# A recurrence and a gated MLP on one core: x through DRAM, state copies on ScalarE, u on four tiles, paired lane groups, and an order that counts queue time

## The chip, the cores and the metric

The kernel runs on one core of a Trainium2 chip. The core has five engines with a queue of instructions each: TensorE (PE; its weight loads are shown as PEld), VectorE (DVE), ScalarE (ACT), GpSimd (POOL) and SyncE (SP). Here SP issues every DMA. The metric is the device time of one execution in microseconds; the time before is the median of three runs.

## What is computed

Two parts in a row. First a recurrence over 768 tokens, for 4 batches and 8 heads of dimension 40:

```python
for t in range(S):
    y[:, :, t] = np.einsum('bhd,bhde->bhe', rt, state)
    Sa = np.einsum('bhde,bhe->bhd', state, at)
    state_decay = state * wt[:, :, None, :] - np.einsum('bhd,bhe->bhde', Sa, bt)
    state = state_decay + np.einsum('bhd,bhe->bhde', vt, kt)
```

Then y, reshaped to x of 3072 tokens by 320, goes through a gated product: `a = x @ w_a; b = x @ w_b; out = (a * b) @ w_out`, with d_ff = 1536. All in float32; the weights come in a wide form that is decoded on the chip.

## The kernel before

**Chunks.** The 768 tokens are cut into 12 chunks of 64 (`C`). A chunk is worked on in two pairs c = 0, 1 (two batches each, `NP`), so there are 24 steps. In a chunk the recurrence is solved with matrices, in these stages:

- `prep(n, c)` (line 506) loads w, b/k and a (tiles W, BK, A), scales them by running products on DVE (Q, pe), makes the `scores` on PE, copies them to AB and TK, and transposes BK (`nat`, tile bkn). A, pe, TK and bkn are written to a DRAM tensor `un_d[q]`.
- `lanes(g)` (line 600) inverts the triangular 32 x 32 blocks of a group of chunks: one transposition of AB, 31 steps of two DVE operations on tiles Y, Yt and N, two transpositions back. `GROUPS` (line 40) says which chunks share one such inverse; a group costs the same whether it holds one chunk or two. `merge` (line 632) completes the inverse of a chunk, tile T; four DMAs copy its diagonal blocks (`T<-TC`).
- `main(n, c)` (line 687) is the step itself. It loads UN (all of `un_d[q]` in one transfer), v into half of SV, and r and v (RV). On PE: `r_`, `u_` (line 716; u in two layouts), `s_`, `g_`, `y_`, and a transposition of the state. On ACT and DVE the results go to RH, SV, uT, tmp, ST, G, SD. `s0` (line 752) copies the state ST to SV for the next chunk by four DMAs of 40 partitions. Last, DVE makes X (one buffer), ACT rounds it to XH, POOL forms the rest X - XH in X.
- `packh` and `packl` (lines 797, 804) move XH and X into the K-tiles `xk` of the second part, 120 partitions with three heads each, by six DMAs each from SBUF to SBUF.

**The second part.** One `unit` (line 410) is one chunk with one of the 12 weight tiles of 128 columns of d_ff: 16 matmuls into ab, a product on DVE, a split on ACT and POOL (gh, gl), 6 matmuls into po. The first four weight tiles (`F1`) are used chunk by chunk beside the recurrence. Each xk is also written to `xk_d[n]`; when the recurrence's buffers are free, all xk and the partial sums (`po_d`) are loaded again and the other eight tiles run over all chunks.

**What sets the order.** The code does not run its steps as written. `Plan.op` (line 84) notes each with its engine, an assumed length, its tiles and a rank v; `Plan.run` (line 116) places them: again and again, of the operations that could start earliest, the one of lowest rank is emitted. Each engine then runs what it was given, in that order. Every DMA is planned on SP with a length of 0.06 (0.12 to 0.36 for several) and a fixed time to landing of 2.5 to 5, whatever else is under way:

```python
pl.op("SP", 0.06, lambda: nc.sync.dma_start(out=UN, in_=un_d[q]), [("un", q, i) for i in range(5)], [kU], lat=4.0, v=v - 0.3)
pl.op("SP", 0.24, s0, [kST], [kS], lat=2.6)
pl.op("SP", 0.36, packh, [kXH], [("xkh", n % 2, c)], lat=2.6, v=v + 0.15)
```

All engine calls pass through one helper, so in the profile nearly every instruction carries line 58; the tiles' names tell them apart.

Of the kernel before, what the change touches and what calls it, by code (L numbers as in the profile page):

```python
# [18 lines left out]
B = 4  # L19
H = 8  # L20
D = 40
# [3 lines left out]
M = 8  # L25
# [14 lines left out]
GROUPS = ((0,), (1, 2), (3, 4), (5, 6), (7, 8), (9, 10), (11,))  # L40
# [4 lines left out]
KHEADS = ((0, 1, 6), (2, 3, 7), (4, 5))  # L45
# [18 lines left out]
class Op:  # L64
    __slots__ = ("eng", "dur", "fn", "deps", "users", "v", "lat", "need", "free", "mode", "end", "left", "ready", "seq")
# [9 lines left out]
class Plan:  # L75
# [40 lines left out]
    def run(self, slack=0.05, switch=0.13):  # L116
        engines = {e: 0.0 for e in ("PE", "DVE", "ACT", "POOL", "SP", "-")}
        busy = dict.fromkeys(engines, 0.0)
# [10 lines left out]
        while todo:  # L129
# [126 lines left out]
def wkv_moe(ctx, tc, wd, ai, bk, rvf, vn, pin, rv, wa, wb, wo, out):  # L256
# [48 lines left out]
    xk_d = [dram.tile([PK, 6, B * C], F32, name=f"xk_d{n}") for n in range(NS)]  # L305
    po_d = [dram.tile([2, P, DM], F32, name=f"po_d{n}") for n in range(NS)]
# [19 lines left out]
    def decode(i, src, rows, ncol, dst_hi, dst_lo, split):  # L326
# [10 lines left out]
        if not WIDE:  # L337
            yield "SP", 0.06, lambda: nc.sync.dma_start(out=raw, in_=src), (), (kr,), 3.0
# [7 lines left out]
        yield "SP", 0.06, lambda: nc.sync.dma_start(  # L346
            out=raw.rearrange("p c x -> p (c x)"), in_=src.bitcast(I32)), (), (kr,), 3.5
# [44 lines left out]
    def plan_tile(f, w, slot, v):  # L392
        for i, j, (eng, dur, fn, r, wr, lat) in tile_steps(f, w):
            kw = {"lat": lat} if lat else {}
# [5 lines left out]
        pl.op("SP", 0.12, lambda: fill_rows(w[0]), [("wt", slot, j) for j in range(2)],  # L400
              [("wf", slot)], v=v, lat=2.5)
# [79 lines left out]
    RH_ = ring(a1, 2, [P, M, D], "RH")  # L481
# [5 lines left out]
    XH_ = ring(a1, 1, [P, 4, 2 * C], "XH", F32R)  # L487
# [3 lines left out]
    for t in (AB, *T_, *ST_, *SV_, D1):  # L491
# [14 lines left out]
    def prep(n, c, v):  # L506
# [4 lines left out]
        un = un_d[q]  # L511
# [3 lines left out]
        pl.op("SP", 0.06, lambda: nc.sync.dma_start(out=W, in_=wd[n, c]), w=[kW], lat=2.6)  # L515
        pl.op("SP", 0.06, lambda: nc.sync.dma_start(out=BK.rearrange("p m x t -> p (m x t)"), in_=bk[n, c]), w=[kBK], lat=3.5)
        pl.op("SP", 0.06, lambda: nc.sync.dma_start(out=A.rearrange("p m t -> p (m t)"), in_=ai[n, c]), w=[kA], lat=2.6)
# [28 lines left out]
        def ak(gq):  # L546
            for j in range(2):
                nc.sync.dma_start(out=AKd[half(gq), gq, j],
                                  in_=A[half(j), gq * 4:gq * 4 + 4].rearrange("p i t -> p (i t)"))
        for gq in range(2):  # L550
            pl.op("SP", 0.12, lambda gq=gq: ak(gq), [kA], [("un", q, gq)], lat=2.6, v=v + 0.3)
        pl.op("SP", 0.06, lambda: nc.sync.dma_start(
            out=un[:, 16 * C:16 * C + CW], in_=PEt.rearrange("p m t -> p (m t)")), [kPE], [("un", q, 2)], lat=2.6, v=v + 0.3)
# [3 lines left out]
        def scores(ps=ps):  # L557
            for i in range(4):
                for kind in range(2):
                    for gq in range(2):  # L560
                        for j in range(2):
                            m, r = mi(gq, i), hd(j)
                            c0 = (kind * 4 + i) * C
                            mul(AT[half(gq ^ kind), ps.first + j, c0:c0 + C], BK[r, m, gq ^ kind], A[r, m])
        pl.op("PE", 1.86, scores, [kBK, kA], need=ps, mode="q", lat=0.1, w=[("sc", q), kAB, kTK])
# [17 lines left out]
        pl.op("SP", 0.12, tk, [kTK], [("un", q, 3)], lat=2.6, v=v + 0.3)  # L583
# [7 lines left out]
        pl.op("PE", 0.86, nat, [kBK], need=ps, mode="t", lat=0.1, w=[("nt", q), kBN])  # L591
# [4 lines left out]
        pl.op("SP", 0.06, lambda: nc.sync.dma_start(  # L596
            out=un[:, 16 * C + CW:], in_=BN.rearrange("p m j d -> p (m j d)")), [kBN], [("un", q, 4)], lat=2.6, v=v + 0.3)
# [34 lines left out]
    def merge(n, x, v):  # L632
# [16 lines left out]
        else:  # L649
            pl.op("SP", 0.24, diag, [("TC", x)], kT[0:2], lat=5.0)  # L650
# [7 lines left out]
        pl.op("PE", 1.05, l2a, kab + [("T3", x)], [("l3", n), "W4"], need=ps, mode="h", lat=0.1)  # L658
# [13 lines left out]
        pl.op("PE", 1.05, l2b, ["W4", ("TC", x)], [("l4", n), kT[2]], need=ps, mode="h", lat=0.1)  # L672
# [7 lines left out]
    def load_v(n, c, v):  # L680

        def go():
            for h in range(2):
                nc.sync.dma_start(out=SV_[c][half(h), 1 - h].rearrange("p j i d -> p (j i d)"), in_=vn[n, c, half(h)])
        pl.op("SP", 0.12, go, w=[("svv", c)], lat=2.6, v=v)

    def main(n, c, v):
# [7 lines left out]
        pl.op("SP", 0.06, lambda: nc.sync.dma_start(out=UN, in_=un_d[q]), [("un", q, i) for i in range(5)], [kU], lat=4.0, v=v - 0.3)  # L695
# [4 lines left out]
        pl.op("SP", 0.06, lambda: nc.sync.dma_start(  # L700
            out=RV.rearrange("p x m t -> p (x m t)"), in_=rvf[n, c]), w=[kRV], lat=3.0, v=v - 0.2)
# [3 lines left out]
        def r_(ps=ps):  # L705
            for j in range(2):
                for i in range(4):
                    for gq in range(2):
                        k = (j * 4 + i) * D
                        mul(AT[half(gq), ps.first, k:k + D], AK[:, gq, j, i], SV[:, gq, j, i])  # L710
        pl.op("PE", 0.95, r_, [kS, kV, kU], [("r", q), kRH], need=ps, mode="c", lat=0.1)
        pl.op("ACT", act(320), lambda ps=ps: nc.scalar.mul(
            out=RH.rearrange("p m d -> p (m d)"), in_=bank(ps, 0, slice(0, 8 * D)), mul=-1.0), [("r", q)], [kRH], free=[ps])
        ps = Banks(2)

        def u_(ps=ps):
            for m in range(M):
                for h in range(2):
                    mul(AT[half(h), ps.first, m * D:(m + 1) * D], T[half(h), m], RH[half(h), m])
            for m in range(M):  # L720
                for h in range(2):
                    mul(AT[hd(h), ps.first + 1, m * C:(m + 1) * C], RH[half(h), m], T[half(h), m])
        pl.op("PE", 1.86, u_, [kRH, *kT], [("u", q), kS, "ut"], need=ps, mode="q", lat=0.1)
        for h in range(2):
            pl.op("ACT", act(320), lambda h=h, ps=ps: nc.scalar.copy(
                out=SV[half(h), h].rearrange("p j i d -> p (j i d)"), in_=AT[half(h), ps.first, 0:8 * D]),
                [("u", q)], [kS])
        pl.op("ACT", act(512), lambda ps=ps: nc.scalar.copy(
            out=UT.rearrange("p m t -> p (m t)"), in_=bank(ps, 1)), [("u", q), kS], ["ut"], free=[ps], v=v + 0.05)
        if n < NS - 1:  # L730
# [9 lines left out]
            pl.op("PE", 0.62, s_, [kU, kS, kV], [("s", q), kST, "tmp"], need=ps, mode="c", lat=0.1)  # L740
# [11 lines left out]
            def s0():  # L752
                for gq in range(2):
                    for j in range(2):
                        nc.sync.dma_start(out=SV[hd(gq), gq, j], in_=ST[hd(j), :, gq, 0:D])
            pl.op("SP", 0.24, s0, [kST], [kS], lat=2.6)

        ps = Banks(2)

        def g_(ps=ps):  # L760
            for m in range(M):
                for kind in range(2):
                    for gq in range(2):
                        l = RV[hd(gq), 1, m] if kind else UT[hd(gq), m]
                        mul(AT[half(gq ^ kind), ps.first + gq, m * C:(m + 1) * C], l, RV[hd(gq), 0, m])
        pl.op("PE", 1.86, g_, ["ut", kRV], [("gs", q), "g"], need=ps, mode="q", lat=0.1, v=v + 0.1)
# [36 lines left out]

        def packl():
# [396 lines left out]
```

## Time and profile before

| what | us |
|---|---|
| time before, median of 3 runs (1172.13 to 1179.04) | 1177.94 |
| the profiled execution, its time | 1175.14 |
| the profiled execution, its span | 1173.4 |
| busy in the span: PE, PEld | 832.9, 774.4 |
| busy in the span: DVE, ACT, POOL | 593.9, 336.8, 230.3 |
| mean granted TensorE clock | 0.796 |
| DMA: packets, bytes | 117389, 152.58 MB |

A span is the time from the first to the last instruction of the profiled execution. Busy time counts an engine's instructions, not its waiting, and leaves out the issuing of DMAs. A group's row gives the operation, the tiles it writes and reads, shape and count, then busy time, the mean length in ns, and the idle time ahead of it with what ended it. The chain of waits goes back from the last instruction, step by step, to what released each; in it SPq is the time in which SP issues a DMA, and a DMA piece is the time from an issue to its landing.

### The profile page before, as it was taken

Reading aid. Unit: us, or ns where it says so; the run is one execution under the profiler, and the core shown is the slowest. Engines: PE = TensorE matmul, PEld = TensorE weight load, DVE = VectorE, ACT = ScalarE, POOL = GpSimd, SP = SyncE. Lnnn points to the kernel's source line nnn. Section 1 sums busy time; section 2 is a strip of 40 time slices with the busy share of each in tenths; the row PEclk is TensorE's granted clock in tenths of the full one; section 3 lists DMA queues with packets and bytes.
Section 4 is the critical chain, followed back from the end, with each engine's and each line's share of the span. In section 5 each row is a group of like instructions: output and inputs, shape, how many; then the busy total and the mean of one; then the engine's idle time right before and its main releaser. Section 6 shows DMA issues by size and latency. Waiting matters only on the chain. (4 is left out here: it accounts for less than half of the span.)

```text
span 1173.4 us, 29555 instructions
## 1 busy us (share of the span) xinstructions
PE 832.9 (71%) x12538; PEld 774.4 (66%) x12538; DVE 593.9 (51%) x1179; ACT 336.8 (29%) x795; POOL 230.3 (20%) x267
## 2 busy tenths in 40 slices
PE   1424566767766877766776577764882999999997
PEld 1424455656655766665675576663781999999997
DVE  6597665457564561167332577413732975322222
ACT  2333123232342232223332133122321443222222
POOL 1012221101100010101000011012441664222222
PEclk9999566567855575877676878576995999999999
DMA  7861435573764555454645453457377220000011
GB/s 226 274 207 54 150 77 159 179 239 118 224 163 137 175 149 161 146 168 147 157 133 155 140 145 95 120 184 175 89 187 180 75 56 15 1 2 1 23 57 59
DMA packets 117389, 152.58 MB, mean 130 GB/s; under 512 B 48498, under 2 KB 85618, under 8 KB 114178
## 3 DMA queue, kind: packets, MB, share of 16 engines
q1 hardware_dynamic: 117250, 150.62, 43.8%
q8 instruction: 100, 1.64, 0.6%
q14 instruction: 39, 0.32, 0.1%
HBM read 93.12 MB, written 42.48 MB: 116 GB/s over the span
## 5 line engine op out<-in xcount | busy, mean ns | idle before, releaser
L58 PE MATMUL ab<-xk,wt 120*128 120x256 f32 x2304 | 346.4, 303 | 46.6 <-DVE g L58 36.5
L58 PEld LDWEIGHTS ab<-xk,wt 120*128 120x128 f32 x2304 | 320.1, 207 | 56.8 <-DVE g L58 41.0
L58 POOL TENSOR_TENSOR gl<-g,gh 128x256 fp32r<-128x256 f32 x144 | 114.4, 795 | 486.2 <-ACT gh L58 470.5
L58 PE MATMUL po<-wo,gh 128*128 128x320 f32 x576 | 163.5, 332 | 18.9 <-ACT gh L58 15.8
L58 DVE TENSOR_TENSOR g<-ab,asb 128x256 f32<-128x256 f32 x144 | 60.5, 421 | 184.4 <-ACT asb L58 184.1
L58 PEld LDWEIGHTS po<-wo,gh 128*128 128x128 f32 x576 | 109.6, 201 | 22.8 <-ACT gh L58 17.0
L58 PE MATMUL AT<-SV,un 128*64 128x40 f32 (+1 forms) x1472 | 63.4, 259 | 76.5 <-ACT uT L58 18.7
L58 PEld LDWEIGHTS AT<-SV,un 128*64 128x64 f32 (+1 forms) x1472 | 57.6, 172 | 85.8 <-issue 27.3
L58 ACT COPY asb<-ab 128x256 f32<-128x256 f32 x144 | 53.6, 372 | 174.2 <-PE ab L58 173.6
L58 PE MATMUL po<-wo,gl 128*128 128x320 f32 x288 | 95.2, 331 | 3.9 <-POOL gl L58 3.6
L58 ACT CAST gh<-g 128x256 fp32r<-128x256 f32 x144 | 58.4, 406 | 99.3 <-DVE g L58 99.2
L58 DVE TENSOR_TENSOR Yt<-Y,N 128x31 f32<-128x31 f32 (+15 forms) x217 | 85.9, 396 | 1.9
L58 DVE TENSOR_TENSOR Y<-Y,Yt 128x31 f32<-128x31 f32 (+15 forms) x217 | 80.3, 370 | 7.5
L58 POOL TENSOR_TENSOR X<-X,XH 128x512 fp32r<-128x512 f32 x24 | 33.3, 1389 | 236.8 <-ACT XH L58 170.1
L58 PE MATMUL AT<-ident,BK 128*128 128x128 f32 x192 | 40.5, 381 | 41.1 <-DVE TK L58 13.9
L58 PEld LDWEIGHTS po<-wo,gl 128*128 128x128 f32 x288 | 58.4, 203 | 7.7 <-POOL gl L58 7.6
L58 PEld LDWEIGHTS AT<-ident,BK 128*128 128x128 f32 x192 | 33.4, 199 | 44.0 <-issue 23.1
L58 PE MATMUL AT<-RH,T 64*64 64x40 f32 x768 | 40.7, 281 | 24.0 <-DVE G L58 7.1
L58 DVE TENSOR_TENSOR X<-AT,un 128x512 f32<-128x512 f32 x24 | 16.6, 690 | 79.3 <-DMA xk<-X 34.4
L58 PEld LDWEIGHTS AT<-RH,T 64*64 64x64 f32 x768 | 37.4, 194 | 29.1 <-DVE G L58 7.7
L58 DVE TENSOR_TENSOR BK<-BK,Q 128x1024 f32<-128x1024 f32 x24 | 29.2, 1215 | 45.1 <-DMA BK<-in_bk_dram 45.1
L58 POOL TENSOR_TENSOR w_mt<-w_mt,wt 120x384 f32<-120x384 f32 x24 | 26.6, 1110 | 128.9 <-ACT wt L58 128.9
(83 smaller groups left out, 1180.2 us busy)
## 6 DMA issues: line engine op xcount, KB each, us to landing
un<-un_d SPq DMA_DIRECT2D x24, 1092.0 KB
BK<-in_bk_dram SPq DMA_DIRECT2D x24, 512.0 KB
rv<-in_rvf_dram SPq DMA_DIRECT2D x24, 512.0 KB
xk_d<-xk SPq DMA_DIRECT2D x11, 720.0 KB
xk<-xk_d SPq DMA_DIRECT2D x11, 720.0 KB
un_d<-bkn SPq DMA_DIRECT2D x24, 320.0 KB
W<-in_wd_dram SPq DMA_DIRECT2D x24, 260.5 KB
un_d<-pe SPq DMA_DIRECT2D x24, 260.0 KB
```

The costliest lines, as they stand in the source:

```text
L58: r = fn(*args, **kwargs)
```

## The change

Five edits, and a planner that counts differently:

- **Lane groups.** `GROUPS` holds six pairs of chunks; before, chunks 0 and 11 had a group each.
- **x through DRAM.** XH and the twelve packing DMAs of a step are gone. X is written to a DRAM tensor `x_d[n]` by one DMA a step. After both steps of a chunk, three DMAs of 40 partitions read it into a tile XF in the order of the K-tiles, and ACT and POOL split it there. Five transfers a chunk in place of 24.
- **State.** `s0` becomes four ACT copies of 64 partitions x 160 at the head of the next step. v is loaded as a tile of 128 partitions with zeros in the half that the state overwrites, one DMA instead of two, twice the bytes; it writes all of SV.
- **u on four tiles.** The 64 matmuls of `u_` alternate over four 64 x 64 tiles of PE (row half and column half change each time), with two PSUM banks; before, each run of 32 used two tiles. `r_` and the copies from PSUM follow that layout. In `scores`, `g_` and `y_` the rows go from 40 to 64, with zeros.
- **A.** Four DMAs that write A to `un_d` become two.
- **The planner.** `pl.dma` plans a DMA on SP with a length of about 0.42 and a share of one ring that all transfers pass, one after another. Lengths of several PE steps change too.
- With this the heads are dealt to the K-tiles in another order (`KHEADS`, `fill_rows`), and RH is widened and cleared in place of SV.

```diff
-GROUPS = ((0,), (1, 2), (3, 4), (5, 6), (7, 8), (9, 10), (11,))
+GROUPS = ((0, 1), (2, 3), (4, 5), (6, 7), (8, 9), (10, 11))
...
+    def dma(self, fn, r, w, moved, dur=0.42, v=None):
+        return self.op("SP", dur, fn, r, w, v=v, moved=moved)
...
+            if o.moved:
+                ring = max(ring, s + 0.3) + o.moved
+                o.end = max(s + d, ring) + 1.8
...
-        pl.op("SP", 0.12, go, w=[("svv", c)], lat=2.6, v=v)
+        pl.dma(lambda: nc.sync.dma_start(out=SV_[c].rearrange("p g j i d -> p (g j i d)"), in_=vn[n, c]),
+               [], [("svv", c), ("svs", c)], 1.1, v=v)
...
+            def s0(gq):
+                for j in range(2):
+                    nc.scalar.copy(out=SV[half(gq), gq, j], in_=ST[half(j), :, gq, 0:D])
+            for gq in range(2):
+                pl.op("ACT", 2 * act(160), lambda gq=gq: s0(gq), [kST, kV], [("svs", c)], v=v - 0.05)
...
-            for m in range(M):
-                for h in range(2):
-                    mul(AT[half(h), ps.first, m * D:(m + 1) * D], T[half(h), m], RH[half(h), m])
-            for m in range(M):
-                for h in range(2):
-                    mul(AT[hd(h), ps.first + 1, m * C:(m + 1) * C], RH[half(h), m], T[half(h), m])
-        pl.op("PE", 1.86, u_, [kRH, *kT], [("u", q), kS, "ut"], need=ps, mode="q", lat=0.1)
+            for i in range(4):
+                for x in range(2):
+                    for gq in range(2):
+                        for j in range(2):
+                            m, h = j * 4 + i, half(gq ^ j)
+                            if x:
+                                c0 = 4 * D + i * C
+                                mul(AT[half(gq), ps.first + j, c0:c0 + C], RH[h, m], T[h, m])
+                            else:
+                                mul(AT[half(gq), ps.first + j, i * D:(i + 1) * D], T[h, m], RH[h, m, 0:D])
+        pl.op("PE", 1.3, u_, [kRH, *kT], [("u", q), kS, "ut"], need=ps, mode="q", lat=0.1)
...
-        pl.op("SP", 0.36, packh, [kXH], [("xkh", n % 2, c)], lat=2.6, v=v + 0.15)
-        pl.op("SP", 0.36, packl, [kX], [("xkl", n % 2, c)], lat=2.6, v=v + 0.15)
+        pl.dma(lambda: nc.sync.dma_start(out=x_d[n][:, :, c].rearrange("g p t -> p g t"), in_=X), [kX], [("xd", n, c)], 0.9, v=v + 0.15)
...
+        def rows(j):
+            nc.sync.dma_start(out=XF[(j + 1) * D:(j + 2) * D, 0:3], in_=x[hd(j), 3:0:-1])
+        def first():
+            w = B * C
+            a = x[hd(0), 0]
+            nc.sync.dma_start(
+                out=XF[0:D], in_=bass.AP(tensor=a.tensor, offset=a.offset, ap=[[w, D], [C * w, 4], [1, w]]))
+        for j in range(2):
+            pl.dma(lambda j=j: rows(j), r, [(*kXF, j)], 0.5, 0.8, v=v)
+        pl.dma(first, r, [(*kXF, 2)], 0.6, 0.8, v=v)
+        kf = [(*kXF, i) for i in range(3)]
+        k = ("xk", n % 2)
+        pl.op("ACT", act(512), lambda: nc.scalar.copy(out=xk[:, 0:2], in_=XF[:, 0:2]), kf, [k + (0,)], v=v)
+        pl.op("POOL", 1.3, lambda: nc.gpsimd.tensor_sub(out=xk[:, 3:5], in0=XF[:, 0:2], in1=xf[:, 0:2]), kf + [k + (0,)], [k + (1,)], v=v)
+        def last():
+            nc.scalar.copy(out=xk[:, 2:6:3], in_=XF[:, 2:3].to_broadcast([PK, 2, B * C]))
+            nc.scalar.copy(out=xk[0:D, 5], in_=XF[0:D, 3])
+        pl.op("ACT", act(512) + act(256), last, kf, [k + (2,)], v=v)
+        pl.op("POOL", 1.3, lambda: nc.gpsimd.tensor_sub(
+            out=xk[0:D, 2:6:3], in0=XF[0:D, 2:4], in1=xf[0:D, 2:6:3]), kf, [k + (2,)], v=v)
```

Three places in the order show what moves. A number behind a name is a buffer's. The first is SP around the second pair of chunk 0. Before, the state's four DMAs, the loads of r/v and un, and then the packs:

```order
L58 DMA SV1_192<-in_vn_dram 64x320 x2
L58 DMA wraw1_145<-in_wb_dram 120x768
L58 DMA SV1_192<-ST1_200 40x4x40 x4
L58 DMA rv1_194<-in_rvf_dram 128x1024
L58 DMA un1_188<-un_d3_114 128x2184
L58 DMA xk0_206<-XH0_205 40x3x128
L58 DMA xk0_206<-XH0_205 40x128 x2
```

The last two rows come once more for the other half, then four of their kind from X. On the same engine, of the change:

```order
L58 DMA SV1_204<-in_vn_dram 128x640
L58 DMA rv1_206<-in_rvf_dram 128x1024
L58 DMA x_d0_99<-X0_216 128x4x128
L58 DMA un1_200<-un_d3_126 128x2184
L58 DMA XF_217<-x_d0_99 40x3x256 x2
L58 DMA XF_217<-x_d0_99 40x4x256
L58 DMA SV0_203<-in_vn_dram 128x640
```

The state's DMAs are gone, and one write of X stands where the twelve packs of a step stood.

The second is PE at the first unit (ab) of chunk 0. Before, it stands one step (r, the row of SV and un) behind the last y of that chunk (the row of G and un):

```order
L58 MATMUL AT_63<-G_198,un1_188 40x64 x16
L58 MATMUL AT_63<-ident_68,ST1_200 128x128 x4
L58 MATMUL AT_63<-SV1_192,un1_188 64x40 x16
L58 MATMUL ab0_64<-xk0_206,wt0_216 128x256 x8
L58 MATMUL ab1_65<-xk0_206,wt1_218 128x256 x8
```

Of the change, it stands behind the first pair's y of chunk 1 and the u of chunk 1's second pair (rows of RH and T, which now alternate):

```order
L58 MATMUL AT_63<-G_210,un0_199 40x64 x16
L58 MATMUL AT_63<-RH1_209,T1_202 64x40 x4
L58 MATMUL AT_63<-T1_202,RH1_209 64x64 x4
...
L58 MATMUL AT_63<-ident_68,ST0_211 128x128 x4
L58 MATMUL ab0_64<-xk0_218,wt0_228 128x256 x8
L58 MATMUL AT_63<-SV1_204,un1_200 40x40 x16
```

More work of the recurrence stands ahead of the first use of x. Counted over the whole order, 44.5 of the 144 units stand ahead of the last y before and 41.5 with the change.

The third is DVE where the first inverse begins (the transposition of AB to N). Before, after two preparations:

```order
L58 SCALAR_TENSOR_TENSOR w_rs0_148<-w_rs0_148,w_ex0_146 120x384
L58 TENSOR_TENSOR TK0_176<-AT_63,tri_76 128x512
L58 STREAM_TRANSPOSE N_181<-AB_180 128x32x32
L58 TENSOR_TENSOR BK1_173<-BK1_173,Q1_169 128x1024
L58 TENSOR_TENSOR Yt_183<-Y_182,N_181 128x31
```

Of the change, after four (three of the rows of TK stand ahead of this one's):

```order
L58 TENSOR_TENSOR BK0_184<-BK0_184,Q0_180 128x1024
L58 TENSOR_TENSOR A0_186<-A0_186,pe0_189 128x512
L58 TENSOR_TENSOR w_mt1_162<-w_ex1_161,w_mt1_162 128x320
L58 SCALAR_TENSOR_TENSOR w_rs1_163<-w_rs1_163,w_ex1_161 128x320
L58 TENSOR_TENSOR TK0_188<-AT_63,tri_76 128x512
L58 STREAM_TRANSPOSE N_193<-AB_192 128x32x32
```

The first inverse is DVE's row 83 in place of 38: two more preparations and more decoding of weights stand ahead of it.

More of the change, by code (lines that the diff above doesn't have):

```diff
@@ L64 @@
 class Op:
-    __slots__ = ("eng", "dur", "fn", "deps", "users", "v", "lat", "need", "free", "mode", "end", "left", "ready", "seq")
+    __slots__ = ("eng", "dur", "fn", "deps", "users", "v", "lat", "need", "free", "mode", "end", "left", "ready", "seq", "moved")
 class Banks:
@@ L305, in wkv_moe @@
     xk_d = [dram.tile([PK, 6, B * C], F32, name=f"xk_d{n}") for n in range(NS)]
+    x_d = [dram.tile([4, P, NP, 2 * C], F32, name=f"x_d{n}") for n in range(NS)]
     po_d = [dram.tile([2, P, DM], F32, name=f"po_d{n}") for n in range(NS)]
@@ L486, in wkv_moe @@
     X_ = ring(a1, 1, [P, 4, 2 * C], "X")
[L487 removed]
+    XF = a1.tile([PK, 4, B * C], F32, name="XF")
     XK_ = ring(mp, 2, [PK, 6, B * C], "xk", F32R)
[L491 removed]
+    for t in (AB, *T_, *ST_, *RH_, D1):
         nc0.vector.memset(t, 0.0)
@@ L543, in size, with ak @@
                     accum_out=sizes[:, 2 * q + i:2 * q + i + 1])
[L546 to L553, printed above, removed]
+        def ak(j):
+            a = AKd[half(0), 0, j]
+            nc.sync.dma_start(
+                out=bass.AP(tensor=a.tensor, offset=a.offset, ap=[[UW, C], [C * UW + 8 * C, 2], [1, 4 * C]]),
+                in_=A[half(j)].rearrange("p (g i) t -> p g (i t)", g=2))
+        for j in range(2):
+            pl.dma(lambda j=j: ak(j), [kA], [("un", q, j)], 0.45, 0.55, v=v + 0.3)
+        pl.dma(lambda: nc.sync.dma_start(
+            out=un[:, 16 * C:16 * C + CW], in_=PEt.rearrange("p m t -> p (m t)")), [kPE], [("un", q, 2)], 0.9, v=v + 0.3)
         ps = Banks(2)
@@ L694, in main @@
         kU, kT = ("U", q % NU), [("T", n % NT, i) for i in range(3)]
-        pl.op("SP", 0.06, lambda: nc.sync.dma_start(out=UN, in_=un_d[q]), [("un", q, i) for i in range(5)], [kU], lat=4.0, v=v - 0.3)
+        pl.dma(lambda: nc.sync.dma_start(out=UN, in_=un_d[q]), [("un", q, i) for i in range(5)], [kU], 3.7, v=v - 0.3)
         SV, RV, RH = SV_[c], RV_[c], RH_[q % 2]
@@ L709, in r_ @@
                         k = (j * 4 + i) * D
-                        mul(AT[half(gq), ps.first, k:k + D], AK[:, gq, j, i], SV[:, gq, j, i])
-        pl.op("PE", 0.95, r_, [kS, kV, kU], [("r", q), kRH], need=ps, mode="c", lat=0.1)
+                        mul(AT[half(gq ^ j), ps.first, k:k + D], AK[:, gq, j, i], SV[:, gq, j, i])
+        pl.op("PE", 1.05, r_, [kS, kV, kU], [("r", q), kRH], need=ps, mode="c", lat=0.1)
         pl.op("ACT", act(320), lambda ps=ps: nc.scalar.mul(
-            out=RH.rearrange("p m d -> p (m d)"), in_=bank(ps, 0, slice(0, 8 * D)), mul=-1.0), [("r", q)], [kRH], free=[ps])
+            out=RH[:, :, 0:D], in_=bank(ps, 0, slice(0, 8 * D)).rearrange("p (m d) -> p m d", d=D), mul=-1.0), [("r", q)], [kRH], free=[ps])
@@ L923, in wkv_moe @@
               + [(k, c) for k in ("svs", "svv", "rv", "rh", "st", "sd") for c in range(NP)]
-              + ["ut", "g", "tmp", ("x", 0), ("xh", 0)])
+              + ["ut", "g", "tmp", ("x", 0)] + [("xf", 0, i) for i in range(3)])
     def late():
@@ L1145, in layout @@
     rvf = np.concatenate([dchannel(r), dchannel(v)], -1)
-    hv = heads(v)
-    vn = hv.transpose(0, 1, 2, 6, 4, 3, 5, 7)[:, :, ::-1].reshape(ns, NP, P, DM)
+    hv = heads(v).transpose(0, 1, 2, 6, 4, 3, 5, 7).reshape(ns, NP, 2, C, DM)
+    vn = np.zeros((ns, NP, 2, C, 2, DM), np.float32)
+    for g in range(2):
+        vn[:, :, 1 - g, :, g] = hv[:, :, g]
+    vn = vn.reshape(ns, NP, P, 2 * DM)
     order = [h for t in KHEADS for h in t]
     def pack(x, fill):
-        x = np.concatenate([x[:, order], np.full((B, 1, S, D), fill, np.float32)], 1)
+        x = np.concatenate([x[:, order[:6]], np.full((B, 1, S, D), fill, np.float32), x[:, order[6:]]], 1)
         return x.reshape(B, NG, 3, ns, C, D).transpose(3, 0, 2, 5, 1, 4).reshape(ns, B, PK, NG, C)
```

155 lines of the change are left out of this document (67 added, 88 removed).

## The prediction

> **What bounds the kernel now.** I read the stretches first. Each row gives a stretch, then the busy time of the engines (with instruction counts), the granted TensorE clock, the share of the DMA engines and GB/s.
>
> ```profile
> 0.00:105.00 105.00, 34.84 (x688) 30.83 (x688) 80.72 (x158) 33.75 (x76) 12.64 (x25) 1.00 0.65 203
> ...
> 105.00:860.00 755.00, 519.92 (x9721) 470.42 (x9722) 381.86 (x734) 213.24 (x492) 105.28 (x109) 0.70 0.51 149
> 860.00:905.00 45.00, 18.54 (x140) 17.96 (x139) 11.77 (x25) 7.68 (x21) 12.10 (x14) 0.76 0.91 222
> 905.00:1173.40 268.40, 259.63 (x1993) 255.17 (x1991) 119.53 (x263) 82.11 (x208) 100.27 (x120) 0.98 0.11 33
> ```
>
> The columns are PE, PEld, DVE, ACT, POOL. From 905 us on, PE is busy 97% and is the bound. The stage from 105 to 860 us, which holds the recurrence and the first weight tiles, is different: PE 69%, DVE 51%, DMA engines 51%. Nothing computes all the time there, so I read who issues. These rows are one tile's DMA issues on the SP queue (min/median/max in ns), and the X product that ends each pair's step:
>
> ```profile
> L58 SPq DMA_DIRECT2D xk<-XH x144: 706/760/1412, 117.8 to 853.9; - x144
> L58 SPq DMA_DIRECT2D xk<-X x144: 706/731/1172, 122.6 to 859.0; - x144
> L58 DVE TENSOR_TENSOR X<-AT,un x24: 679/691/693, 116.4 to 848.4; 128x512 f32<-128x512 f32 x24
> L58 SPq DMA_DIRECT2D SV<-ST x88: 767/786/2208, 109.7 to 782.0; - x88
> L58 SPq DMA_DIRECT2D un_d<-A x96: 445/594/1769, 20.6 to 652.4; - x96
> L58 SPq DMA_DIRECT2D SV<-in_vn_dram x48: 466/582/1766, 9.1 to 778.7; - x48
> L58 SPq DMA_DIRECT2D un_d<-bkn x24: 320/390/1422, 16.5 to 704.7; - x24
> ```
>
> A transfer of 40 partitions holds the queue 0.73 to 0.79 us, one of 128 partitions 0.39. The packing alone is 144 x 0.760 + 144 x 0.731 = 214.7 us of one queue that every other transfer shares. Whether this ends anything is told by the chain of waits, here for 605 to 860 us (back to where the chain begins), then pieces of it around one pair, then the queue's timeline there:
>
> ```profile
> by line: SPq L58 19.6%; PE AT L58 13.6%; issue 11.0%; DMA un<-un_d 9.6%; PE ab L58 6.2%; DMA xk<-X 5.2%; PE po L58 3.9%; DMA xk<-XH 3.0%; DMA wraw<-in_wo_dram 2.5%; DMA A<-in_ai_dram 2.4%; DVE w_ex L58 2.2%; DVE w_rs L58 2.0%; DVE G L58 1.8
> ```
>
> ```profile
> 664.72 0.80 SPq L58
> ...
> 672.83 0.73 SPq L58
> ...
> 673.60 1.84 DMA xk<-X
> ...
> 675.57 0.69 DVE X L58
> ...
> 676.28 7.59 DMA un<-un_d
> ```
>
> ```profile
> 660.64 3.44 SPq L58 DMA_DIRECT2D SV<-ST  x4
> ...
> 664.72 4.77 SPq L58 DMA_DIRECT2D xk<-XH  x6
> 669.59 4.72 SPq L58 DMA_DIRECT2D xk<-X  x6
> ...
> 676.28 0.33 SPq L58 DMA_DIRECT2D un<-un_d  x1
> ```
>
> Twelve issues in a row (4.77 + 4.72 = 9.49 us) must go out and land (1.84) before the one X buffer is free; the next X is made in 0.69; only then may the buffer of un be refilled, and that load stands behind the packs in the same queue. PE has 13.6 + 6.2 + 3.9 = 24% of this chain, SP's issuing 19.6%. So the stage is bound by the round of one queue and two single buffers, not by an engine.
>
> **The change part by part**, against the profiled execution (span 1173.4; its time 1175.14 lies 1.74 above the span and 2.8 below the median of the runs).
>
> *Packing.* 288 issues go. In their place come 24 writes of X from 128 partitions (0.390 like bkn: 9.4 us) and 36 reads into 40 partitions (at most 0.786: 28.3 us). On the path: SPq is 19.6% of 255 us = 50 us; matched by start time with the queue's rows, 36 us of them are pack issues. The landings xk<-X and xk<-XH add 8.2% = 21 us. So 57 of 255 us, 22%, and over 755 us 168. What comes back is the write and its landing before X is free, 0.39 + 1.84 = 2.2 us for each of 24, 53 us if always on the path; I take half. That gives -140. Ends: -215, the whole issue time, and -60, if the chain before 605 us, which no view shows, held a third of that.
>
> The reads, two ACT copies and two POOL subtractions a chunk now follow both pairs. ACT and POOL work stays about equal, by these rows:
>
> ```profile
> L58 ACT CAST XH<-X 128x512 fp32r<-128x512 f32 x24 | 14.9, 620 | 68.9 <-DVE X L58 58.4 <-DMA SV<-in_vn_dram 10.5
> L58 POOL TENSOR_TENSOR X<-X,XH 128x512 fp32r<-128x512 f32 x24 | 33.3, 1389 | 236.8 <-ACT XH L58 170.1 <-DMA SV<-ST 36.5 <-DMA un_d<-bkn 20.3
> L58 ACT COPY SD<-AT 128x320 f32<-128x320 f32 x22 | 9.4, 425 | 32.2 <-PE AT L58 16.9 <-DVE X L58 10.8 <-DVE tmp L58 3.0
> L58 ACT COPY pcs<-Q 128x8 f32<-128x8 f32 x24 | 4.9, 203 | 41.4 <-DVE Q L58 41.3
> ```
>
> They are costed at nothing because the order puts other PE work ahead of the first unit that needs x: the first ab of chunk 0 now stands behind the u step of chunk 1's second pair, not right behind the last y. If that cover is gone, it is the third rival.
>
> *State.* 88 issues x 0.786 = 69 us leave the queue. Four ACT copies of 160 elements a pair take their place, between 0.203 and 0.425 each, so about 0.31: 22 x 1.24 = 27 us of ACT, on the recurrence. Before, four issues (3.44 us) and a landing stood there, the landing in a piece of the same chain:
>
> ```profile
> 723.70 2.01 DMA SV<-ST
> ```
>
> But the load of v now fills the whole SV tile, so it waits until the step's last read of SV and stands in that place. I take 0, between -26 (their 8.9 us of the chain's 255, by the same matching, over the stage) and +27.
>
> *A and v.* 96 issues become 48 (-28.5 us), 48 become 24 of 128 partitions (48 x 0.582 - 24 x 0.390 = -18.6). By the same matching they hold 4.4 of the 255 us: 13 over the stage. I take -10 (0 to -47).
>
> *u on four tiles.* Matmul rows of u before, and of scores, which has as many instructions and already alternates tiles:
>
> ```profile
> L58 PE MATMUL AT<-RH,T 64*64 64x40 f32 x768 | 40.7, 281 | 24.0 <-DVE G L58 7.1 <-DVE TK L58 6.0 <-DVE X L58 3.2
> L58 PE MATMUL AT<-A,BK 40*64 40x64 f32 x1536 | 39.2, 275 | 15.8 <-ACT w_ex L58 5.0 <-ACT bkn L58 3.5 <-ACT W L58 2.3
> L58 PE MATMUL AT<-T,RH 64*40 64x64 f32 x768 | 38.8, 276 | 0.0
> ```
>
> u takes 40.7 + 38.8 = 79.5 us and would take 39.2: -40 of PE. PE is busy 69% of the stage and has 24% of the chain, so about a third counts: -15 (0 to -40). Scores, g and y were planned at other lengths, but their tiles were already so; they get nothing.
>
> The Trainium skill's page "TensorEngine Tiling (Array Packing)", Restrictions and Gotchas, says that different row tiles cannot use one PSUM bank at a time. In the new u both row tiles write each bank. By that rule the -15 is 0 and the sum below 15 higher. The trace does not decide it: the old u, whose two row tiles also shared a bank, ran at half the rate of scores, whose row tiles have a bank each (the rows above), but it also used two tiles, not four.
>
> *Lane groups, seven to six.* Update and transpose rows of one group's inverse:
>
> ```profile
> L58 DVE TENSOR_TENSOR Yt<-Y,N 128x31 f32<-128x31 f32 (+15 forms) x217 | 85.9, 396 | 1.9
> L58 DVE TENSOR_TENSOR Y<-Y,Yt 128x31 f32<-128x31 f32 (+15 forms) x217 | 80.3, 370 | 7.5
> L58 DVE STREAM_TRANSPOSE N<-AB 128x1024 f32<-128x1024 f32 x7 | 14.7, 2107 | 0.0
> L58 DVE STREAM_TRANSPOSE TC<-Y 128x1024 f32<-128x1024 f32 x7 | 14.7, 2102 | 0.1
> L58 DVE STREAM_TRANSPOSE T<-Y 128x1024 f32<-128x1024 f32 x7 | 13.4, 1912 | 0.0
> ```
>
> (85.9 + 80.3 + 14.7 + 14.7 + 13.4) / 7 = 29.9 us of DVE a group. DVE is busy 80.72 of the first 105 us, so one group less is -30. Against it, four preparations instead of two stand ahead of the first group: the first chunk starts later, the second no longer waits for a group of its own. Ends: 0, if the later start eats it, and -60, if the rounds of the first and the last chunk's own groups both leave the path.
>
> *Order by queue times.* In the stage SP waits too, and what stands behind it waits with it:
>
> ```profile
> SPq L58 <- PE AT L58: 57.4, 19, 10.6
> ```
>
> An order that knows the queue's length can avoid part of it: -15 (0 to -57).
>
> *End.* Three more units lie behind the last y in the order. A unit is 22 matmuls, 259.63 x 22 / 1993 = 2.87 us: +9.
>
> Sum: -140 + 0 - 10 - 15 - 30 - 15 + 9 = -201. 1173.4 - 201 = 972.4, and with 1.74 **974 us**.
>
> **Rivals.**
>
> *PE's floor.* All that SP holds up goes, order included. The stage then cannot fall under PE's 519.92 - 40 = 480 us: 755 - 480 = 275 less, some 22 at the start, 9 back: about 887. For it: DVE's 382 us and the DMA engines' 0.51 x 755 = 385 lie below. Against: steps also wait for each other across engines, and an order in which each engine takes them one by one keeps much of that, as here in the stage:
>
> ```profile
> ACT SV L58 <- PE AT L58: 51.0, 18, 10.4
> ```
>
> *Issuing is hidden anyway.* When the packs go, the next chain, of un's landing (7.59) and in-order waits, ends a little sooner only. Then the groups, u and a little of the order are left: -30 - 15 - 13 + 9 = -49, 1126 us. For it: SP itself waits 57.4 us for PE. Against: the twelve issues seen in the chain.
>
> The skill's page "DMA: Bandwidth & Descriptors", Issuing engines are not separate DMA queues, has it that starting a DMA takes a sequencer little time beside the transfer; by that rule this rival would hold. The trace disagrees: 9.49 us of issuing stand before 1.84 of landing.
>
> *x comes late (slower).* PE runs in order. If its first unit on a chunk's x waits for the way out, back and the splits, the next recurrence step behind it waits as well. The way has two landings, 1.84 to 7.59 each, then 0.62 + 1.39 twice: 8 to 19 us. It outweighs the rest only if PE stands 17 us or more a chunk (201 / 12); at the full 19, 12 x 19 - 201 = +27, some 1202.
>
> **Chances.** Forecast 0.63, PE's floor 0.17, hidden 0.12, late x 0.05, and 0.03 that gains and such waits cancel. 974 is the likeliest case's time; its own range by the bounds that can go together is 915 to 1050. The range reaches to the floor with some room, 870, and up to 1075 for packs at -60 with the rest small (1175 - 60 - 10 - 15 - 30 + 9 = 1069). Outside lie 0.12 + 0.05 + 0.03. A change of about 1% is what a measurement of this kernel can tell from none: faster 0.92, same 0.03, slower 0.05.
>
> **What would show it.** Right: SP's issues of x number 60 and hold the queue under 40 us in all; X no longer waits for a DMA of xk; the chain has SPq under 8%; six transposes of AB; the matmuls of u take about 40 us; X's 24 rows end some 190 us earlier, and the last 268 us look as before. Wrong: PE waiting for POOL's or ACT's write of xk before ab; DVE or ACT waiting long for SV's load; un's landing taking the chain's freed share; or the granted clock in the stage falling under 0.70.

## The result and the profile after

| what | before | after |
|---|---|---|
| time, median (runs) | 1176.41 (4; 1172.13 to 1179.04) | 1010.43 (4; 1007.98 to 1010.82) |
| span of the profiled execution | 1173.4 | 1006.3 |
| DMA packets | 117389 | 98945 |

The ratio is 0.8588, with a 95% interval of 0.8557 to 0.8619: 166 us less, where 201 were forecast. 1010 lies in the range (870 to 1075) and in the likeliest case's own (915 to 1050), 36 us above the 974 forecast.

The stretches of the changed kernel, with the columns of the stretches shown before:

```profile
0.00:105.00 105.00, 34.94 (x640) 30.25 (x640) 91.28 (x167) 38.20 (x91) 21.46 (x30) 0.95 0.79 259
105.00:700.00 595.00, 430.03 (x9696) 386.10 (x9697) 348.95 (x658) 234.91 (x565) 93.69 (x97) 0.76 0.62 186
700.00:750.00 50.00, 41.70 (x314) 40.79 (x314) 16.95 (x37) 15.69 (x41) 21.76 (x25) 0.94 0.83 192
750.00:1006.30 256.30, 245.64 (x1892) 240.91 (x1890) 120.85 (x254) 78.46 (x199) 93.40 (x114) 0.99 0.11 35
```

The stage of the recurrence took 595 us in place of 755, at a PE share of 72% in place of 69%. These 160 us are nearly all of the 167 us by which the span is shorter. Next, rows of X, x_d, XF and SV by tile (min/median/max ns of one, first and last start):

```profile
L58 DVE TENSOR_TENSOR X<-AT,un x24: 681/691/692, 140.5 to 691.9; 128x512 f32<-128x512 f32 x24
L58 SPq DMA_DIRECT2D x_d<-X x24: 370/378/999, 141.2 to 692.6; - x24
L58 SPq DMA_DIRECT2D XF<-x_d x36: 286/349/1597, 154.4 to 695.8; - x36
L58 SPq DMA_DIRECT2D SV<-in_vn_dram x24: 328/352/1738, 3.6 to 650.2; - x24
```

The 60 transfers of x hold SP for 24 x 0.378 + 36 x 0.349 = 21.6 us, where the 288 held it for 214.7. The last X is made at 691.9 instead of 848.4, but the first at 140.5 instead of 116.4. The chain of waits over the stage (105 to 700 us), by line:

```profile
by line: PE AT L58 40.3%; PE ab L58 6.0%; issue 5.6%; DVE Yt L58 4.5%; DVE G L58 4.1%; ACT SV L58 3.9%; DVE Y L58 3.6%; DVE X L58 2.3%; ACT W L58 2.3%; ACT uT L58 2.1%; DVE T L58 1.8%; PE po L58 1.8%; ACT AB L58 1.7%; ACT T L58 1.7%; DVE tm
```

SPq, 19.6% of the chain before (which covers the last 255 us of its stage only), is not among the lines shown any more, so under 1.7%, nor is a landing. PE's matmuls into AT, ab and po make 48% in place of 24%: a step now runs from engine to engine, with PE the largest part. Two groups show that the new way of x and the new copies of the state are covered (busy us, mean ns, idle time before and what ended it):

```profile
L58 PE MATMUL ab<-xk,wt 120*128 120x256 f32 x2304 | 323.2, 292 | 16.7 <-DVE g L58 12.5 <-ACT xk L58 1.5 <-POOL xk L58 1.3
L58 ACT COPY SV<-ST 64x160 f32<-64x160 f32 x88 | 28.4, 323 | 4.7 <-DMA SV<-in_vn_dram 3.6
```

PE waited 2.8 us in all for an xk, and ACT 3.6 us for v.

The granted clock of the stage rose too, from 0.70 to 0.76, and PE was busy 430 us there in place of 520 for nearly the same number of matmuls. Among them those of ab kept PE busy 0.158 us each (111.94 us for 710) in place of 0.187 (142.67 for 765). That a higher clock made the gain does not fit the runs: ten executions of the kernel before with other planned lengths (the second part of the experiments) had a mean clock of 0.763 to 0.770 in four and 0.808 to 0.824 in six, and took 1171.5 and 1170.9 us in the mean.

### The profile page after: what moved, and what is told of

It reads as the page before. It is cut to its first block, busy times and chain, and to the rows that moved or that the text cites. A ratio compares the mean times of both kernels' runs of the same rounds, so it can differ in the third digit from the quotient of the medians.

```text
span 1006.3 us, 28951 instructions
## 1 busy us (share of the span) xinstructions
PE 752.3 (75%) x12538; PEld 698.1 (69%) x12538; DVE 578.0 (57%) x1114; ACT 367.3 (36%) x895; POOL 230.3 (23%) x265
## 2 busy tenths in 40 slices
DMA packets 98945, 156.57 MB, mean 156 GB/s; under 512 B 30250, under 2 KB 64106, under 8 KB 95738
## 4 chain that ended last, share of the span: by engine, by line
PE 48%; DVE 25%; ACT 11%; DMA 7%; issue 5%; SPq 1%; POOL 1%; DVEq 0%; POOLq 0%; ACTq 0%
PE AT L58 25%; PE ab L58 16%; PE po L58 7%; DVE Yt L58 3%; DVE Y L58 3%; DVE G L58 2%; ACT SV L58 2%; DMA xk<-xk_d 2%; DVE g L58 2%; DVE w_ex L58 2%; DMA wraw<-in_wb_dram 2%; DVE w_mt L58 2%; DVE w_rs L58 2%; ACT W L58 1%; ACT AB L58 1%
## 5 line engine op out<-in xcount | busy, mean ns | idle before, releaser
L58 PE MATMUL ab<-xk,wt 120*128 120x256 f32 x2304 | 323.2, 292 | 16.7 <-DVE g L58 12.5
L58 PEld LDWEIGHTS ab<-xk,wt 120*128 120x128 f32 x2304 | 301.8, 197 | 23.8 <-DVE g L58 17.5
L58 PE MATMUL po<-wo,gh 128*128 128x320 f32 x576 | 155.5, 318 | 5.1 <-ACT gh L58 3.8
L58 DVE TENSOR_TENSOR Y<-Y,Yt 128x31 f32<-128x31 f32 (+15 forms) x186 | 70.4, 378 | 6.4
L58 DVE TENSOR_TENSOR Yt<-Y,N 128x31 f32<-128x31 f32 (+15 forms) x186 | 72.1, 388 | 1.5
L58 POOL TENSOR_TENSOR xk<-XF,xk 120x512 fp32r<-120x512 f32 (+1 forms) x24 | 32.4, 1368 | 175.2 <-ACT xk L58 175.2
L58 DVE TENSOR_TENSOR tmp<-AT,ST 128x320 f32<-128x320 f32 x20 | 9.8, 492 | 78.8 <-PE AT L58 51.3
L58 PE MATMUL AT<-A,BK 64*64 64x64 f32 x1536 | 39.3, 274 | 13.7 <-ACT bkn L58 5.5
L58 PEld LDWEIGHTS AT<-A,BK 64*64 64x64 f32 x1536 | 35.4, 183 | 19.0 <-ACT bkn L58 6.9
L58 PE MATMUL AT<-rv,uT 64*64 64x64 f32 x768 | 37.2, 265 | 13.5 <-DVE tmp L58 5.0
(84 smaller groups left out, 1173.4 us busy)
```

The lines of the kernel that those rows point to most:

```text
L58: r = fn(*args, **kwargs)
```

## Experiments

Each edit starts from the kernel before or from the changed one; the expectation says which. Ratios are to the kernel before on the same chip, whose medians there were 1172.6, 1171.97 and 1170.34 us. A difference from the changed kernel is taken from its 1010.43 us, which were measured beside 1176.41; taken by the ratios, each comes out 2 to 7 us higher.

### The queue and its packs

**x through DRAM alone**, on the kernel before, with nothing else of the change but the order of heads that it needs:

```diff
-        pl.op("SP", 0.36, packh, [kXH], [("xkh", n % 2, c)], lat=2.6, v=v + 0.15)
-        pl.op("SP", 0.36, packl, [kX], [("xkl", n % 2, c)], lat=2.6, v=v + 0.15)
+        pl.op("SP", 0.06, lambda: nc.sync.dma_start(out=x_d[n][:, :, c].rearrange("g p t -> p g t"), in_=X), [kX], [("xd", n, c)], lat=2.6, v=v + 0.15)
...
+            pack(n, n + 0.3)
```

> The kernel before with one part of the change: x goes out through DRAM and comes back in three reads; lane groups, state, u and the order's queue lengths are as before. Theory (the packs' 288 issues and the held X buffer are the path): about 1176 - 140 = 1036, at least 1080 or less. Rival 1 (issuing is hidden behind other waits): within 15 us of 1176. Rival 2 (the order that knows the queue made the gain, not the transfers): 1150 or more.

1083.59 us, ratio 0.9222 (0.917 to 0.9274): 89 us less, just short of what the theory asked for (1080). Its rows by tile, and the chain from 605 to 760 us, the stretch before its last X:

```profile
L58 DVE TENSOR_TENSOR X<-AT,un x24: 675/692/693, 117.5 to 761.6; 128x512 f32<-128x512 f32 x24
L58 SPq DMA_DIRECT2D x_d<-X x24: 370/383/660, 118.2 to 762.4; - x24
L58 SPq DMA_DIRECT2D XF<-x_d x36: 295/342/846, 135.2 to 765.4; - x36
```

```profile
by line: PE AT L58 25.4%; DMA wraw<-in_wo_dram 8.4%; PE ab L58 7.1%; SPq L58 4.8%; DVE Yt L58 4.7%; issue 4.4%; PE po L58 3.8%; DVE w_ex L58 3.2%; DVE G L58 3.1%; DVE Y L58 3.1%; DMA wraw<-in_wa_dram 3.1%; DMA XF<-x_d 2.9%; DVE TC L58 2.8%;
```

SP loses 214.7 - (24 x 0.383 + 36 x 0.342) = 193 us of issuing and the kernel 89: 0.46 us for each. SPq falls from 19.6% to 4.8% of the chain, as forecast, and the gain is still 51 us short of 140. Where it is missing is shown by the 15th X, here of the kernel before and then of this one, from their DVE timelines:

```profile
604.88 0.68 DVE L58 TENSOR_TENSOR X<-AT,un 128x512 f32<-128x512 f32 x1
```

```profile
568.21 0.69 DVE L58 TENSOR_TENSOR X<-AT,un 128x512 f32<-128x512 f32 x1 [4.60 <-PE AT L58]
```

From the 15th X to the last the time went from 243.5 us to 193.4, 21% less; from the first to the 15th from 488.5 to 450.7, 8% less.

**A second X and XH**, on the kernel before, so that a new X need not wait for the packs:

```diff
-    X_ = ring(a1, 1, [P, 4, 2 * C], "X")
+    X_ = ring(a1, 2, [P, 4, 2 * C], "X")
-    XH_ = ring(a1, 1, [P, 4, 2 * C], "XH", F32R)
+    XH_ = ring(a1, 2, [P, 4, 2 * C], "XH", F32R)
...
```

> The kernel before with two buffers each for X and XH, one for each pair; all twelve pack transfers a step stay. Theory: the queue's issuing stays, only the wait of the next X for the landing goes, 8.2% of the chain: 1115 to 1165. If the buffer alone is the cause: 1060 or less. Rival 1 (hidden): within 15 us of 1176.

1163.68 us, ratio 0.9925 (0.9881 to 0.997): 9 us, at the edge of the theory's range and within that of rival 1 as well. This wait of the kernel before, in the list of what the engines idled for ahead of X (us, times), is not in this kernel's list any more:

```profile
  DMA xk<-X: 34.4, 7
```

It went and little came of it. So the one buffer alone was not the bound.

**Idle transfers, first form**, on the changed kernel: twelve transfers of 40 partitions behind each write of x, all into one scratch tile, planned at 0.72 us in all:

```diff
...
+        def extra():
+            for k in range(12):
+                s = slice(C * (k % 2), C * (k % 2) + D)
+                nc.sync.dma_start(out=scr[s, :], in_=ident[s, :])
+        pl.op("SP", 0.72, extra, [kX], ["scr"], lat=2.6, v=v + 0.15)
```

> The changed kernel with twelve idle DMAs a step (40 partitions, constant to a scratch tile that nobody reads) behind the write of X, planned at 0.72 us as the packs were; they hold no buffer. Theory: the queue's issue time comes back without the held buffer, 24 x 9 = 216 us of it, half or so on the path: 1075 to 1130. Rival 1 (hidden): 1010 to 1030.

1196.19 us, ratio 1.0201 (1.0151 to 1.025): 186 us more than the changed kernel and above the expected range. SP's waits in the stage tell why this does not separate issuing from landing:

```profile
SPq L58 <- DMA scr<-ident: 100.2, 119, 7.9
```

As all twelve write the same place, SP also stood 100.2 us for landings. The next run removes that.

**Idle transfers, second form**: the same, into six tiles in turn, so that none waits for another:

```diff
-                nc.sync.dma_start(out=scr[s, :], in_=ident[s, :])
+                nc.sync.dma_start(out=scr[k // 2][s, :], in_=ident[s, :])
```

> The changed kernel with twelve idle transfers of 40 partitions after each write of x, this time into six tiles of their own in turn, so that none waits for the one before; they are planned at 0.72 us in all. They hold SP's queue about 12 x 0.75 = 9 us a step, 216 us over 24 steps. If it is the holding of the queue that costs (the theory: taking 204 us of it away was worth 89 us), between 1090 and 1180 us. If the landings and the waits for them were the cost (the rival), under 1030 us, since nothing waits for these.

1104.64 us, ratio 0.9453 (0.9397 to 0.9509): 94 us more than the changed kernel, with nothing that reads what these transfers bring. Their row, and the chain over the last 100 us of its stage:

```profile
L58 SPq DMA_DIRECT2D scr<-ident x288: 706/707/1335, 141.6 to 793.4; - x144
```

```profile
by line: SPq L58 21.4%; issue 17.2%; PE AT L58 15.9%; DMA rv<-in_rvf_dram 8.0%; DMA un<-un_d 5.2%; PE ab L58 4.5%; POOL w_mt L58 3.9%; DMA wraw<-in_wo_dram 3.3%; POOL xk L58 2.6%; ACT T L58 2.4%; DVE G L58 2.3%; POOL wt L58 2.1%; DVE w_ex L
```

288 x 0.707 = 204 us of issuing cost 94: 0.46 us for each, the price at which it was taken away. That the two prices agree so closely is in part chance: x through DRAM alone also took away the packs' landings. SPq is back at 21.4%, or 15.3% from 650 us on, near where this chain begins. What stands behind the bursts in the queue comes late: PE waited 47.8 us for loads of un, where it waited 5.2 in the changed kernel. So holding the queue in bursts is enough to cost this much, with no use of what the transfers bring. Not separated from it are the 5.9 MB that these transfers move (162.49 MB in all, 156.57 in the changed kernel).

### The order

**Lengths on SP alone**, on the kernel before: each DMA is planned at its measured issue time, landings as they were.

```diff
+        if eng == "SP":
+            dur = {0.06: 0.42, 0.12: 1.2, 0.24: 3.2, 0.36: 4.8}[dur]
```

> The kernel before, with only the planned lengths of SP's entries set to what the trace shows (0.42 for one, 1.2, 3.2 and 4.8 for two, four and six transfers); the same transfers, another order. Theory (transfers, not order): 1145 to 1180. Rival 2 (the order made the gain): 1060 or less.

1170.69 us, ratio 0.998 (0.9954 to 1.0006): 2 us, none that can be told from zero.

**The changed kernel planned as before**: its transfers with the old lengths and fixed landing times.

```diff
+        if moved:
+            dur, lat = 0.06 if dur < 0.43 else 0.12, {3.7: 4.0, 2.6: 5.0, 1.2: 3.5, 1.7: 3.5, 2.4: 3.0}.get(moved, 2.6)
+            moved = 0.0
```

> The changed kernel with every DMA planned as before (0.06 or 0.12 us on SP, fixed landing), so another order of the same instructions. Theory (the order is a small term, 15 us): 1010 to 1040. Rival 2 (the order made the gain): 1100 or more.

1063.83 us, ratio 0.9065 (0.8991 to 0.9139): 53 us more, between the theory's range and the rival's. Landings of five kinds make 18% of its chain from 500 to 750 us. Among the longest pieces there are these, and SP's timeline shows what stood ahead of the longest; the third view is the stretch in which it landed (columns as before):

```profile
580.55 7.26 DMA A<-in_ai_dram
...
670.97 15.32 DMA SV<-in_vn_dram
707.89 7.64 DMA un<-un_d
```

```profile
666.21 2.90 SPq L58 DMA_DIRECT2D xk<-xk_d  x4
670.97 0.36 SPq L58 DMA_DIRECT2D SV<-in_vn_dram  x1
```

```profile
671.00:687.00 16.00, 6.68 (x192) 6.11 (x192) 2.92 (x6) 2.14 (x5) 0.00 (x0) 0.61 0.89 215
```

v for the next step was issued in 0.36 us but landed 15.32 us later, behind four reloads of xk for the second part and two loads of weights, while the DMA engines were 89% busy and PE fell to 6.68 of 16 us. The changed kernel issues four such reloads right behind a load of v instead. SP's timeline shows this first; the second view is the longest landing in its chain up to the last X:

```profile
634.17 0.35 SPq L58 DMA_DIRECT2D SV<-in_vn_dram  x1
634.57 1.82 SPq L58 DMA_DIRECT2D xk<-xk_d  x4
```

```profile
478.58 6.07 DMA un_d<-A
```

**x through DRAM and known lengths**, on the kernel before:

```diff
+        if eng == "SP":
+            dur = {0.06: 0.42, 0.12: 1.2, 0.24: 3.2}[dur]
...
```

> The kernel before with x through DRAM and with SP's transfers planned at their real lengths, no other edit; alone these gave 1083.6 and 1170.7. If the order's 53 us need only the short queue, about 1030 to 1045 us. If they need the other edits (landing times behind one ring, the state off the queue, the groups), 1070 to 1085.

1077.08 us, ratio 0.9218 (0.9176 to 0.926), the same as x through DRAM alone. So the 53 us do not come with the issue lengths alone once the queue is short. Its chain from 500 to 750 us still has long landings, among them these:

```profile
688.12 12.96 DMA XF<-x_d
705.79 9.25 DMA wraw<-in_wa_dram
```

What this plan lacks, of what the changed planner knows, is that transfers land one after another; the two late pieces fit that. But it lacks the other edits too, so it is the likely cause and not a shown one: a plan with the landings alone was not tried.

**Idle transfers, second form, planned at their length** (9.1 in place of 0.72):

```diff
-        pl.op("SP", 0.72, extra, [kX], ["scr"], lat=2.6, v=v + 0.15)
+        pl.op("SP", 9.1, extra, [kX], ["scr"], lat=2.6, v=v + 0.15)
```

> The same idle transfers, planned at their real 9.1 us. If an order that knows the queue can put other transfers ahead of the long hold, 20 us or more below the kernel in which they are planned at 0.72. If a hold of 9 us cannot be got round in any order (as knowing the old lengths was worth 2 us in the kernel before), within 10 us of it.

1072.86 us, ratio 0.9182 (0.9139 to 0.9224): 32 us less than unplanned, 62 more than without them. Here the length alone did help: a known burst of 9 us costs 0.31 us for each it holds, in place of 0.46.

### The other parts, each undone in the changed kernel

**Seven lane groups:**

```diff
-GROUPS = ((0, 1), (2, 3), (4, 5), (6, 7), (8, 9), (10, 11))
+GROUPS = ((0,), (1, 2), (3, 4), (5, 6), (7, 8), (9, 10), (11,))
```

> The changed kernel with the seven lane groups of before (chunks 0 and 11 alone). Theory (a group costs 30 us of DVE that something waits for): 1030 to 1050. Rival (the first chunk's later start ate the gain, 140.5 against 116.4 us for the first X): 1000 to 1015.

997.65 us, ratio 0.8509 (0.8452 to 0.8566): 13 us less than the changed kernel (9 by the ratios, whose intervals overlap a little), under the rival's range too, and the fastest kernel here. Its X row:

```profile
L58 DVE TENSOR_TENSOR X<-AT,un x24: 666/692/693, 103.8 to 682.7; 128x512 f32<-128x512 f32 x24
```

The first X comes 36.7 us sooner than with six groups, the last 9.2 us. From the first X to the last, seven groups take 578.9 us and six 551.4. These 27.5 us fit the 29.9 us of DVE that a group costs, so the saved group seems to give its price there; but with six groups the first step stands behind four preparations and a group of two, and 36.7 us are lost before it.

**u in runs of eight on two tiles:**

```diff
-            for i in range(4):
-                for x in range(2):
-                    for gq in range(2):
-                        for j in range(2):
+            for x in range(2):
+                for j in range(2):
+                    for i in range(4):
+                        for gq in range(2):
```

> The changed kernel with the 64 matmuls of u in runs of eight on two tiles (the two row halves into one bank), the same results. Theory: u takes 2.0 to 3.6 us again in place of 1.16 to 1.98, 40 us of PE, a third to a half of it on the path: 1023 to 1035; by a chain in which PE has half, 1035. Rival (off the path): 1010 to 1015.

1019.33 us, ratio 0.8693 (0.8631 to 0.8755): 9 us more (12 by the ratios), between the theory's range and the rival's. One u of each kind, all at a granted clock of 1.00; from PE's timelines of before, after and this run (start, length, count; in the second the first and the last of eight rows, in the third of ten):

```profile
185.43 1.13 PE L58 MATMUL AT<-RH,T 64*64 64x40 f32 x32
186.38 1.07 PE L58 MATMUL AT<-T,RH 64*40 64x64 f32 x32
```

```profile
250.35 0.33 PE L58 MATMUL AT<-RH,T 64*64 64x40 f32 x8
...
251.19 0.32 PE L58 MATMUL AT<-T,RH 64*64 64x64 f32 x8
```

```profile
252.13 0.75 PE L58 MATMUL AT<-RH,T 64*64 64x40 f32 x26
...
252.83 0.80 PE L58 MATMUL AT<-T,RH 64*64 64x64 f32 x27
```

64 matmuls took 2.02 us before, 1.16 after and 1.51 in this run. Over the 24 steps, first start to last end of each u added up, they took 74.6, 42.1 and 51.7 us: this run has 9.6 us more of u and is 9 us slower. With the same u in other kernels the sum differs a little: it is 40.6 and 39.8 in the next two runs, whose u is the changed one, and 64.4 in the kernel with x through DRAM alone, whose u is the old one.

**The state by four DMAs, v in halves:**

```diff
-                    nc.scalar.copy(out=SV[half(gq), gq, j], in_=ST[half(j), :, gq, 0:D])
...
+                        nc.sync.dma_start(out=SV[hd(gq), gq, j], in_=ST[hd(j), :, gq, 0:D])
...
```

> The changed kernel with the state copied to SV by four DMAs a step and v loaded into its half by two, both planned at their real length. Theory (the two ways cost the same on the path): 1005 to 1025. Rival (the four issues were worth the 8.9 of 255 us of the chain): 1035 or more.

1010.0 us, ratio 0.8602 (0.8528 to 0.8676): no change, as expected.

**A by four transfers:**

```diff
...
-        for j in range(2):
-            pl.dma(lambda j=j: ak(j), [kA], [("un", q, j)], 0.45, 0.55, v=v + 0.3)
+        for gq in range(2):
+            pl.dma(lambda gq=gq: ak(gq), [kA], [("un", q, gq)], 0.45, 1.19, v=v + 0.3)
```

> The changed kernel with A written by four transfers again in place of two. 48 more issues of about 0.6 us, 28 us of queue. If each held microsecond of the queue still costs as the packs' did (89 of 204), about +12: 1022 us. If the queue has slack now, within 4 us of 1010.

1008.37 us, ratio 0.8615 (0.8575 to 0.8655): no change. Its 96 issues hold SP 96 x 0.588 - 48 x 0.610 = 27 us longer than the changed kernel's 48, at no cost:

```profile
L58 SPq DMA_DIRECT2D un_d<-A x96: 445/588/2348, 15.9 to 535.4; - x96
```

```profile
L58 SPq DMA_DIRECT2D un_d<-A x48: 588/610/2203, 17.9 to 531.7; - x48
```

## Why the prediction was right, and where its steps failed

The mechanism and the verdict were right: the stage was bound by one queue's issuing, and it is no longer. The sum was 35 us too large (201 for 166), made of a large term that was too big, one that was too small, and one of the wrong sign, so that the nearness of the total is partly luck.

- **Packing, -140: right in kind, too large; alone it is worth 89.** The share of the chain was sound where it was read: 22% of the last 255 us, and the last 243.5 us became 21% shorter. The failing step is the next one, "over 755 us 168". Up to the 15th X only 8% went. The prediction had no view of the chain there and allowed for that only in the end at -60. Of its two parts, issuing and landing, the wait for the landings gave little by itself: the second buffer took it away and gained 9 us.
- **What comes back of the packing, half of 53 us: not seen as such.** The write of X and its landing are not among the lines shown of the changed kernel's chain. The reads were bounded at 0.786 us and took 0.349.
- **Order, -15: it was worth 53.** It was read from SP's waits for PE (57.4 us, of which a part). The changed order did not shorten these; they grew, as the waits of SP in the stage show, and SP has time to wait now:

```profile
SPq L58 <- PE AT L58: 147.6, 52, 8.5
```

  What the old order loses seems to lie in another place, of which the term took no account: in landings, the longest of them the 15.32 us behind large reloads. That these make the 53 us is argued from the chains and not shown.
- **Lane groups, -30: wrong sign, 9 to 13 us slower than seven.** The prediction named the later start and then let it weigh nothing. The first X moved from 116.4 to 140.5 us, and with seven groups it comes at 103.8. The price of a group fits (27.5 us between the first X and the last), but the start outweighed it.
- **u, -15: probably low.** The one kernel with a slower u lost 9 us (12 by the ratios) for 9.6 us more of u, so PE time here seems to count nearly in full and not by a third. At that rate u on four tiles would be worth some 22 us: of the 32.4 us that u lost (74.6 to 42.1), 10 were gone with x through DRAM alone (64.4), whose u is the old one. The whole undoing of u was not run. By the rule of the Trainium skill's page "TensorEngine Tiling (Array Packing)", Restrictions and Gotchas, that different row tiles cannot access one PSUM bank simultaneously, the prediction took it that the term might be 0; 64 matmuls took 1.16 us in place of 2.02 all the same. This does not refute the rule: in the new loop j chooses the bank and changes with every call, so that two neighbouring calls never write the same bank, while in the old one 32 matmuls in a row write one.
- **State, 0: right.** DMAs or copies, the time is the same. **A and v, -10: 0 for A,** and v's halves, which were undone together with the state, are no loss seen beside it. The share of their issues in the old chain did not survive the packs.
- **End, +9: right as work, but the end became shorter.** These are the stretches from the end of the last X on, before and after:

```profile
849.12:1173.40 324.28, 286.41 (x2178) 281.37 (x2178) 133.41 (x293) 93.80 (x238) 115.84 (x137) 0.94 0.22 60
```

```profile
692.62:1006.30 313.68, 294.72 (x2263) 289.08 (x2261) 139.54 (x294) 96.43 (x245) 116.64 (x141) 0.98 0.23 62
```

PE has 8.3 us more to do there, and stands 19.0 us instead of 37.9, so that this end is 10.6 us shorter.

Added up, 89 for the packing, 53 for the order, 9 for u against runs of eight and -13 for the groups make 138 of the 166 us. Where the other 28 lie is open: the rest of u and the shorter end are candidates. The first term was measured on the kernel before and the others on the changed one, so they need not add up exactly.

The rivals: *PE's floor* was not reached, PE is busy 430 of the stage's 595 us, and PE's and DVE's turns in a step fill the chain instead. Nor were its 480 us a floor: PE's busy time fell by 90 us and not by 40, of which u is 32; the matmuls of ab, shorter beside a higher granted clock, are another part. *Issuing is hidden anyway* fell: 204 us of issuing with nothing behind it cost 94. The rule of the Trainium skill's page "DMA: Bandwidth & Descriptors", Issuing engines are not separate DMA queues, by which starting a transfer usually takes the sequencer little beside the transfer itself, does not fit these of 0.7 us each beside a landing of 1.84. Still there is something in the rival: 27 us of A's issues and 72 of the state's (88 of 0.817) cost nothing. They are planned and spread out, which is the likely reason; no run tests it. *x comes late* did not happen (2.8 us). Of the signs named, all on the right side held but one, X's last rows, which came 157 us earlier and not 190; of the wrong ones none did (the granted clock of the stage rose from 0.70 to 0.76).

## What to carry to other kernels

Price a crowded queue by what it holds in bursts on the path, and check that share in more than one stretch before stretching it over a stage: here it was 21% late and 8% early. Once the queue is free, look at how large transfers are placed ahead of small ones that the next step needs, and give the planner measured durations and landings together: together they were worth 53 us here, the durations alone nothing in two kernels and 32 us where the bursts were long. Work saved on an engine is worth nothing if the start then waits longer for preparation; here the single first chunk was the better choice, and the change with seven groups is the version to keep.

## What was not expected of the hardware

- How long an issue holds SP does not follow from its partitions: 40 partitions from SBUF to SBUF took 0.707 to 0.817 us, 40 partitions from DRAM to SBUF 0.349, as little as 128 partitions (0.352).
- How 64 matmuls of the same work are dealt out changed their time at the same granted clock of 1.00: 2.02 us in runs of 32 on two tiles, each run into one PSUM bank; 1.51 us on two tiles with the bank changing after every eight calls; 1.16 us alternating over four tiles, the bank changing with every call. Which of the two, tiles or banks, does it is not separated.
